# Two decode layers on one core: the MLP in thirds of 1536 columns, with other load orders around it

## The chip, the cores and the metric

The kernel runs on one core of a Trainium2 chip. The metric is the time of one execution on the device in microseconds (us), as the median of several runs. Besides the timed runs there is one profiled execution, from which the trace and the page of the profile come.

## The reference, cut to what matters

All data is float32. A batch of two tokens passes through attention and MLP, twice, with the same weights and the same key and value caches each time.

```python
# x (2, 1, 576); k_cache, v_cache (2, 32, 8192, 128); wq (576, 4096); wo (4096, 576)
# w_gate, w_up (576, 4608); w_down (4608, 576)
def _A_ref(x):
    q = (x @ wq).reshape(2, 1, 32, 128).transpose(0, 2, 1, 3)
    scores = einsum("bhqd,bhkd->bhqk", q, k_cache) * (128 ** -0.5)
    p = softmax(scores, axis=-1)
    o = einsum("bhqk,bhkd->bhqd", p, v_cache)
    return o.transpose(0, 2, 1, 3).reshape(2, 1, 4096) @ wo

def _B_ref(x):
    g = x @ w_gate
    u = x @ w_up
    return (gelu(g, approximate=True) * u) @ w_down

x = x + _A_ref(layernorm(x));  x = x + _B_ref(layernorm(x))
x = x + _A_ref(layernorm(x));  x = x + _B_ref(layernorm(x))
```

The caches hold 537 MB. Both layers together read 1151.6 MB from HBM: the part of the caches that is kept on the chip from layer 0 to layer 1 is read once.

## The kernel before, in words

One large SBUF tile, `space`, takes all that is loaded. The class `Space` manages it while the program is written: every load is a row of `sp.queue` with a key, a place and a length, and `pump` issues the next load on SP's queue as soon as its place holds nothing that is still wanted. `done(key)` marks a load as used and pumps. So the loads come strictly in the order of `sp.queue`, and a load that has to wait for room holds up all that stand behind it. At most eight loads are in flight.

Most of the time is attention over the cache. Layer 0 takes the heads forward, first in pairs, then the last two heads singly; layer 1 takes them backward. For each, DVE multiplies keys by the query (L602), POOL halves the products (L607), DVE reduces them (L621), ACT exponentiates (L674), and PE sums the exponentials (L687) and applies the values (L703).

Two rings in `space` serve the weights. `mid = sp.ring(MID, MIDEND)` has 6912 floats on each partition; through it go, in this order, layer 0's output weights (`out_rows`, 16 loads of 128x1152), its gate and up weights, its down weights, and layer 1's query weights. `big = sp.ring(0, END)` covers the whole tile and serves layer 1's MLP.

The weights that multiply the state (wq, w_gate, w_up) have 576 rows, of which four loads (NW) bring 128 each and a `middle` load brings the 64 that are left. In the MLP the 4608 columns are treated in two halves, and each half in two parts `s`, with 1152 columns to a load (L157, 4608 bytes in a run). `products` (L840) multiplies a block by the state, four matmuls of 288 columns to four 32-row groups of a PSUM bank. `middles` (L189) loads the 64 middle rows of gate and up to alternate partitions of one block, so both are multiplied at once. `hidden` transposes the sums on DVE (L851), applies the norm to them and forms the GELU (L860 to L872). `lower` (L879) multiplies rows of the down weights by it into the PSUM tile `xps`. The down weights come in pieces of some rows each: two rows a load in layer 0 (`first_down`, L200; every ninth row goes with that of the next quarter, L203), and 9, 9, 5, 4, 4, 2, 1, 1, 1 rows in layer 1 (`last_down`). Between the last of these pieces PE does a few products that no result needs (`idle`, L923).

At the end of layer 0's attention `project` (L747) multiplies the output weights, in pieces of two rows. One piece, `early`, stands on PE ahead of the last item's softmax:

```python
early = pieces[:1] if n == last and layer == 0 else []
for piece in early:
    project(*piece)
softmax(n)
total(n)
values(n, pieces[1:9] if n == last and layer == 0 else ())
```

At the start of layer 1 `turn` (L402) transposes the new state, and the query matmuls (L459, L475) run as the query weights land: first those of the last heads, 256 columns (`last_heads`, L169), then two halves in turn. At the end of the program the state is added (L929) and stored (L931).

Of the kernel before, what the change touches and what calls it, by code (L numbers as in the profile page):

```python
# [15 lines left out]
P = 128  # L16
B = 2
# [16 lines left out]
CF = HF // 4  # L34
BF = CF // 2
NI = 9
NT = 4
# [70 lines left out]
def decode_layers(ctx, tc, x_in, kc, vc, wq, wo, wg, wu, wd, out):  # L108
# [74 lines left out]
    def middles(key, where, half, lo=0, hi=HF):  # L183

        def load(a):
            at_of[key] = a
            for r, w in enumerate((wg, wu)):
                src = bass.AP(w.tensor, w.offset + (8 + half) * HF + lo, [[18 * HF, HALF], [1, hi - lo]])
# [49 lines left out]
    idle = {(1, NT - 2, 0): (256, 256), (1, NT - 2, 5): (256, 256, 256), (1, NT - 1, 0): (160,)}  # L238
# [52 lines left out]
    for k in range(1, 4):  # L291
# [3 lines left out]
    cache("k", 1, s0, LATE, 0, 1)  # L295
# [19 lines left out]
    for half in range(2):  # L315
        middles(("m", 1, half), big, half)
# [129 lines left out]
    def attention(layer, items, apart):  # L446
# [25 lines left out]
        else:  # L472
# [7 lines left out]
            nc.vector.memset(qsb[96:P, TAIL:], 0.0)  # L480
            at = at_of["wq", 1, "t"]
# [3 lines left out]
            norm(apart)  # L485
# [3 lines left out]
            qlast = once.tile([P, CT], F32, name="qlast")  # L489
            nc.scalar.activation(qlast, qp[1][:, 0:CT], AF.Copy)  # L490
            apart4 = once.tile([P, 4, B], F32, name="apart4")
            nc.vector.tensor_mul(
                apart4, chosen[:, 1:2, :].to_broadcast([P, 4, B]), quarter.unsqueeze(2).to_broadcast([P, 4, B])
            )
# [23 lines left out]
        def rest_of_queries():  # L518
            for i in range(NW):
# [236 lines left out]
        if layer == 1:  # L756
            body(0)
            body(1)
# [8 lines left out]
        for n in range(last + 1):  # L767
# [4 lines left out]
            for k, unit in enumerate(units):  # L772
# [8 lines left out]
                if k == 0:  # L781
# [6 lines left out]
                    if first:  # L788
                        query(1)
                        first_of_queries()  # L790
                        rest_of_queries()
                    elif n < last:
                        query(n + 1)
                else:
                    add_up(*pending)
                    if k == 1 and layer == 1 and n == 1:
# [10 lines left out]
            if eager(n):  # L807
# [18 lines left out]
        for piece in pieces[9:] if layer == 0 else [(g,) for g in order[3:-1]]:  # L826
# [5 lines left out]
    def mlp(layer, apart):  # L832
        banks = (acc, qp) if layer else ((acc[1], qp[1]), (sm[1], acc[1]))
        done_first = set()

        def products(half, s, lhs, at, stop):
            for c in range(4):
                key = half, s, c
                lo = at + c * BF
                nc.tensor.matmul(  # L840
                    banks[half][s][32 * c:32 * c + WIN, 0:BF], lhs, space[:, lo:lo + BF],
                    start=key not in done_first, stop=stop,
                )
                done_first.add(key)
# [3 lines left out]
        def hidden(half):  # L848
            t = once.tile([P, 2, NI, 32], F32, name="turned", tag="row")
            for s in range(2):  # L850
                nc.vector.transpose(t[:, s, :, :], banks[half][s][:, 0:BF].rearrange("p (j k) -> p k j", k=NI))  # L851
            rows_ = t.rearrange("p s k w -> p (s k) w")[:, :, 0:WIN].rearrange("p t (g r) -> p t g r", g=2)
            shape = [P, 2 * NI, 2, B]
            n = 2 * NI * B
# [11 lines left out]
            h = hT[half] = work.tile([P, 2 * NI, B], F32, name="hT")  # L866
# [7 lines left out]
        def lower(piece):  # L874
            key = ("d", layer) + piece[0]
            for k, (t, i) in enumerate(piece):
                for c in range(4):
                    a = at_of[key] + k * D + c * CW
                    nc.tensor.matmul(  # L879
                        xps[32 * c:32 * c + B, 0:CW], hT[t // 2][:, t % 2 * NI + i, :], space[:, a:a + CW],  # L880
# [5 lines left out]
        if layer == 0:  # L886
            for half in range(2):
                for g, name in enumerate("gu"):
                    for i in range(NW):
                        for s in range(2):  # L890
                            key = name, 0, half, i, s
                            products(half, s, window(g, i), at_of[key], False)
                            done(key)
                        if half == g == i == 0:
# [64 lines left out]
```

## Time and profile before

| what | value |
|---|---|
| median of 3 runs | 2686.24 us (2685.68 to 2686.43) |
| profiled execution, its own time | 2687.66 us |
| its span | 2685.9 us |
| busy share of PE, DVE, ACT, POOL | 35%, 69%, 7%, 43% |
| bytes read from HBM | 1151.60 MB, 429 GB/s over the span |
| share of SP's queue in 16 DMA engines | 99.7% |
| granted TensorE clock, mean | 0.627 |

The span runs from the first to the last recorded instruction; 1.8 us of the execution's time lie outside it. In a row of the page or of the tables, "x8" is a count of instructions, "DMA share" is the mean busy share of the core's 16 DMA engines, and the bracket at the end of a row of the timeline gives how long the engine had been idle and what released it. Layer 0's MLP lies between 1293 and 1370 us of the span, layer 1's from about 2600 us to the end.

### The profile page before, as it was taken

To read this page: it belongs to the slowest core of one execution; us is meant where nothing else is said; L and a number is where in the kernel's file an instruction comes from. 1 tells how busy PE (TensorE), PEld (TensorE's weight loads), DVE (VectorE), ACT (ScalarE), POOL (GpSimd) and SP (SyncE) were. 2 spreads that over 40 slices of the span, in tenths; PEclk is the share of its full clock that TensorE was granted. 3 is DMA by queue.
4 is the path that set the end of the run, shared out by engine and by line. 5 is a ranking of instruction groups with operands and counts; after the bars stand their busy time and mean duration, and the time that the engine had idled before them with its cause. 6 is when DMAs were issued, how large, how long until landed. Compare 5 with 4: busy or idle time off the path is not lost.

```text
span 2685.9 us, 18299 instructions
## 1 busy us (share of the span) xinstructions
PE 940.4 (35%) x7230; PEld 321.6 (12%) x7230; DVE 1863.2 (69%) x1349; ACT 180.5 (7%) x918; POOL 1144.0 (43%) x342
## 2 busy tenths in 40 slices
PE   2332332333233323325764233233323332332346
PEld 0110111011001101102121011001100110111022
DVE  5578777867777687787158777776787778777750
ACT  0000000000000000003013100000000000000000
POOL 2345444544554454453024444554454445445530
PEclk7656665666566566656676566566566656665677
DMA  9999999999999999999999999999999999999998
GB/s 422 435 437 428 434 433 435 434 434 431 432 433 435 434 433 433 431 431 419 407 399 436 433 434 435 433 435 427 436 433 435 432 436 429 434 434 438 426 428 373
DMA packets 38598, 1152.80 MB, mean 429 GB/s; under 512 B 4320, under 2 KB 4976, under 8 KB 17136
## 3 DMA queue, kind: packets, MB, share of 16 engines
q1 hardware_dynamic: 38488, 1151.62, 99.7%
q8 instruction: 57, 0.93, 0.1%
q14 instruction: 29, 0.24, 0.0%
q10 hardware_dynamic: 24, 0.01, 0.0%
HBM read 1151.60 MB, written 0.00 MB: 429 GB/s over the span
## 4 chain that ended last, share of the span: by engine, by line
DMA 26%; DVE 12%; PE 8%; POOL 7%; ACT 1%; issue 1%; POOLq 0%; SPq 0%; ACTq 0%; DVEq 0%
DMA space<-in_A_k_cache_dram 18%; DVE space L602 7%; POOL space L607 7%; PE acc L703 6%; DVE S L621 4%; DMA space<-in_B_w_down_dram 3%; DMA space<-in_A_v_cache_dram 2%; DMA space<-in_B_w_gate_dram 1%; DMA space<-in_B_w_up_dram 1%; DMA space<-in_A_wo_dram 1%; DVE osb L720 1%; ACT prz L674 1%; DMA space<-in_A_wq_dram 1%; PE sm L665 0%; PE sm L684 0%
## 5 line engine op out<-in xcount | busy, mean ns | idle before, releaser
L607 POOL TENSOR_TENSOR space<-space 128x2048 f32<-128x2048 f32 (+3 forms) x332 | 1140.5, 3443 | 1313.9 <-DVE space L602 1180.7
L602 DVE TENSOR_TENSOR space<-space,qp 128x4096 f32<-128x4096 f32 (+2 forms) x329 | 1127.0, 3441 | 462.0 <-DMA space<-in_A_k_cache_dram 451.9
L621 DVE TENSOR_REDUCE S<-space 128x32 f32<-128x2048 f32 (+3 forms) x332 | 582.0, 1753 | 114.9 <-POOL space L607 111.9
L703 PE MATMUL acc<-space,prz 128*8 128x512 f32 x4096 | 593.5, 742 | 7.8 <-issue 6.5
L731 PE MATMUL spare<-weights,osb 128*64 128x2 f32 (+1 forms) x528 | 70.8, 256 | 1198.8 <-ACT osb L722 1181.2
L731 PEld LDWEIGHTS spare<-weights,osb 128*64 128x64 f32 (+1 forms) x528 | 65.2, 208 | 1215.2 <-ACT osb L722 1196.2
L703 PEld LDWEIGHTS acc<-space,prz 128*8 128x8 f32 x4096 | 115.3, 103 | 420.6 <-issue 416.0
L658 PE MATMUL sm<-ident,m 128*1 128x128 f32 x68 | 24.7, 363 | 331.7 <-DVE m L656 331.7
L722 ACT COPY osb<-osb 128x128 f32<-128x128 f32 x60 | 17.9, 298 | 1728.9 <-DVE osb L720 1728.9
L720 DVE SCALAR_TENSOR_TENSOR osb<-acc,diag,osb 128x128 f32<-128x128 f32 x204 | 71.6, 351 | 7.2
L429 POOL TENSOR_TENSOR rstd<-ve,mhalf 128x2 f32<-128x2 f32 x4 | 2.8, 699 | 166.1 <-DVE ve L428 166.1
L684 PE MATMUL sm<-rs,one 128*128 128x2 f32 x120 | 34.8, 360 | 81.1 <-ACT prz L674 81.1
L611 ACT ACTIVATE space<-space 128x128 f32<-128x128 f32 x188 | 55.6, 297 | 69.7 <-DVE space L602 54.8
L674 ACT ACTIVATE prz<-S,nbs 64x128 f32<-64x128 f32 (+1 forms) x136 | 53.3, 392 | 3.1
L665 PE MATMUL sm<-m,one 1*128 1x2 f32 (+1 forms) x136 | 39.0, 354 | 23.0 <-DVE m L663 23.0
L658 PEld LDWEIGHTS sm<-ident,m 128*1 128x1 f32 x68 | 5.4, 79 | 342.4 <-DVE m L656 311.4
L840 PE MATMUL acc<-space,xt 128*6 128x288 f32 x256 | 30.1, 584 | 30.3 <-DMA space<-in_B_w_gate_dram 15.0
L684 PEld LDWEIGHTS sm<-rs,one 128*128 128x128 f32 x120 | 29.7, 307 | 86.3 <-ACT prz L674 86.3
L663 DVE TENSOR_REDUCE m<-sm 1x2 f32<-1x128 f32 (+1 forms) x68 | 18.9, 278 | 30.1 <-PE sm L658 30.1
L851 DVE STREAM_TRANSPOSE turned<-acc 128x288 f32<-128x288 f32 x4 | 1.9, 483 | 52.9 <-PE acc L840 52.9
L665 PEld LDWEIGHTS sm<-m,one 1*128 1x128 f32 x136 | 33.1, 301 | 41.5 <-DVE m L663 41.3
L670 ACT ACTIVATE nbs<-sm 128x2 f32<-128x2 f32 (+1 forms) x68 | 11.7, 172 | 388.5 <-PE sm L665 388.5
(126 smaller groups left out, 432.1 us busy)
## 6 DMA issues: line engine op xcount, KB each, us to landing
space<-in_A_k_cache_dram SPq DMA_DIRECT2D x8, 4096.0 KB, 19.5
space<-in_A_v_cache_dram SPq DMA_DIRECT2D x3, 4096.0 KB, 30.0
space<-in_A_v_cache_dram SPq DMA_DIRECT2D x6, 2048.0 KB, 32.2
space<-in_B_w_down_dram SPq DMA_DIRECT2D x19, 576.0 KB, 7.4
space<-in_B_w_gate_dram SPq DMA_DIRECT2D x18, 576.0 KB, 7.4
space<-in_B_w_up_dram SPq DMA_DIRECT2D x18, 576.0 KB, 7.8
space<-in_A_wo_dram SPq DMA_DIRECT2D x16, 576.0 KB, 8.1
space<-in_A_wo_dram SPq DMA_DIRECT2D x8, 1152.0 KB, 24.0
```

Of the source, the lines that this page charges most:

```text
L602: nc.vector.tensor_tensor(out=u, in0=t, in1=qp_of(n)[:, 0:DH].unsqueeze(1).to_broadcast([P, r1 - r0, DH]), op=ALU.mult)
L607: nc.gpsimd.tensor_tensor(out=half, in0=half, in1=u[:, :r2 - r0, DH // 2:], op=ALU.add)
L611: nc.scalar.activation(row, row, AF.Copy, accum_out=S[n][:, 16 * lo + r:16 * lo + r + 1])
L621: nc.vector.tensor_reduce(out=S[n][:, r0:r1], in_=half, axis=AX.X, op=ALU.add)
L658: nc.tensor.transpose(peaks[n], m, ident)
L665: nc.tensor.matmul(low[n], one[0:1, :].to_broadcast([1, P]), m1, start=True, stop=True)
L674: nc.scalar.activation(prz[rows_, 0:item.rows // 4, e, :], s[rows_, 0:item.rows].rearrange("p (g r) -> p g r", r=4), AF.Exp, bias=nbs[rows ...
L684: nc.tensor.matmul(tot, ones, rs[:, n % 2, :], start=True, stop=True)
L703: nc.tensor.matmul(acc_of(n)[32 * c:32 * c + 8, :], prz[:, g, :, :].rearrange("p e r -> p (e r)"), space[:, at:at + 4 * DH], start=(g < 4) ...
L720: nc.vector.scalar_tensor_tensor(t, q[:, r, :], diag[:, r:r + 1], t, op0=ALU.mult, op1=ALU.add)
L731: nc.tensor.matmul(to[:, i, 0:item.heads], t[:, i:item.heads * DH:GH], w, start=True, stop=True,)
L840: nc.tensor.matmul(banks[half][s][32 * c:32 * c + WIN, 0:BF], lhs, space[:, lo:lo + BF], start=key not in done_first, stop=stop,)
```

## The change

The MLP's columns are taken in three thirds of 1536, each with one PSUM bank, instead of two halves with two banks each. `products` makes four matmuls of 384 columns. `hidden` runs three times in a layer, each with one transpose. Layer 0's gate and up loads have 1536 columns (6144 bytes in a run), its down loads three rows (6912 bytes). Layer 1 loads its middle rows in one key of two loads, and its down weights in pieces of 12, 6, 6, 5, 3, 2, 1, 1 rows; the products between them stand behind the third, fourth and fifth piece. The rings keep their sizes.

Around the MLP three orders change. On PE the output weights' early piece is gone, and the pieces go between the groups of values as 3, 2, 2, 1 instead of 2, 2, 2, 2. In layer 1 the last heads' query weights come behind the first two loads of the body instead of ahead of them, and their products likewise (`tail_queries` behind `body(0)`). One part of the first item's keys is loaded ahead of the last two query loads, and the part that lies in the ring goes ahead of two parts of the next item.

```diff
-NI = 9
-NT = 4
+NT = 3
+NI = 12
+TF = DF // NT
+BF = TF // 4
...
-first_down = []
-for t in (0, 2):
-    for k in range(2):
-        first_down += [run(t + k, lo, lo + 2) for lo in range(0, NI - 1, 2)]
-    first_down.append([(t, NI - 1), (t + 1, NI - 1)])
-last_down = [run(t, 0, 9) for t in range(NT - 2)] + [run(NT - 2, *r) for r in ((0, 5), (5, 9))]
-last_down += [run(NT - 1, *r) for r in ((0, 4), (4, 6), (6, 7), (7, 8), (8, 9))]
+first_down = [run(t, lo, lo + 3) for t in range(NT) for lo in range(0, NI, 3)]
+last_down = [run(*r) for r in ((0, 0, 12), (1, 0, 6), (1, 6, 12), (2, 0, 5), (2, 5, 8), (2, 8, 10), (2, 10, 11), (2, 11, 12))]
...
-for half in range(2):
+for t in range(NT):
     for name, w in (("g", wg), ("u", wu)):
         for i in range(NW):
-            for s in range(2):
-                rows((name, 0, half, i, s), w, HF, mid, (2 * i + half) * HF + s * CF * 2, CF * 2)
-    for s in range(2):
-        middles(("m", 0, half, s), mid, half, s * CF * 2, (s + 1) * CF * 2)
+            rows((name, 0, t, i), w, HF, mid, 2 * i * HF + t * TF, TF)
+    middles(("m", 0, t), mid, t * TF, (t + 1) * TF)
...
-last_heads(("wq", 1, "t"), mid)
-middle(("wq", 1, "tm"), wq, HQ, mid, HQ - TAIL, HQ)
 for half in (1, 0):
     for i in range(NW):
...
+        if half and i == 0:
+            last_heads(("wq", 1, "t"), mid)
+            middle(("wq", 1, "tm"), wq, HQ, mid, HQ - TAIL, HQ)
+        if half == 0 and i == NW - 2:
+            cache("k", 1, s0, LATE, 1, 2)
...
-for k in range(1, 4):
+for k in (2, 3, 0):
     cache("k", 1, s0, LATE, k, k + 1)
 for k in range(2, 4):
     cache("k", 1, s1, home[("k",) + s1.name], k, k + 1, MORE if k == 2 else 0)
-cache("k", 1, s0, LATE, 0, 1)
...
+    counts = [3, 2, 2, 1]
...
-            for piece in between[:2]:
+            count = counts.pop(0) if counts else 0
+            for piece in between[:count]:
                 project(*piece)
-            between = between[2:]
+            between = between[count:]
...
 if layer == 1:
     body(0)
+    tail_queries()
     body(1)
...
-        early = pieces[:1] if n == last and layer == 0 else []
-        for piece in early:
-            project(*piece)
         softmax(n)
         total(n)
-        values(n, pieces[1:9] if n == last and layer == 0 else ())
+        values(n, pieces[:8] if n == last and layer == 0 else ())
...
-    banks = (acc, qp) if layer else ((acc[1], qp[1]), (sm[1], acc[1]))
+    banks = (acc[0], acc[1], qp[0]) if layer else (acc[1], qp[1], sm[1])
...
-            nc.tensor.matmul(sm[0][0:B, 0:n], hT[1][:, 0, :], flat[:, 0:n], start=True, stop=True)
+            nc.tensor.matmul(sm[0][0:B, 0:n], hT[0][:, 0, :], flat[:, 0:n], start=True, stop=True)
```

The first place where this moves instructions is SP's list of loads from the end of layer 0's MLP to the first keys of layer 1. Before, it stands as follows (`space` is the large tile, the names behind the arrow are the tensors in HBM, the shapes count partitions and floats).

```order
L200 DMA space<-in_B_w_down_dram 128x1152 x8
L203 DMA space<-in_B_w_down_dram 128x2x576
L200 DMA space<-in_B_w_down_dram 128x1152 x8
L203 DMA space<-in_B_w_down_dram 128x2x576
L169 DMA space<-in_A_wq_dram 64x4x256 x2
L179 DMA space<-in_A_wq_dram 128x1x256
L157 DMA space<-in_A_wq_dram 128x1x1024
L157 DMA space<-in_A_wq_dram 128x1x768
```

Now it stands so, with the end of the query weights behind the mark.

```order
L200 DMA space<-in_B_w_down_dram 128x1728 x12
L157 DMA space<-in_A_wq_dram 128x1x1024
L157 DMA space<-in_A_wq_dram 128x1x768
L169 DMA space<-in_A_wq_dram 64x4x256 x2
L179 DMA space<-in_A_wq_dram 128x1x256
...
L157 DMA space<-in_A_wq_dram 128x1x1024 x6
L147 DMA space<-in_A_k_cache_dram 128x2048
L157 DMA space<-in_A_wq_dram 128x1x1024 x2
L147 DMA space<-in_A_k_cache_dram 128x2048 x3
```

Eighteen down loads have become twelve, the three loads for the last heads have moved behind the first two loads of the body, and one load of keys has moved ahead of the last two of the query weights.

The second place is PE at the last item of layer 0's attention, where `m` holds the maximum, `rs` the sums of the exponentials, `prz` the exponentials and `oT` the outputs of earlier heads. Before:

```order
L665 MATMUL sm_126<-m_2811,one 128x1
L747 MATMUL xps<-space,oT 2x144 x8
L687 MATMUL sm_126<-rs,one 128x1 x2
L703 MATMUL acc_122<-space,prz 8x512 x4
L747 MATMUL xps<-space,oT 2x144 x16
L703 MATMUL acc_122<-space,prz 8x512 x4
L747 MATMUL xps<-space,oT 2x144 x16
```

And now, where the lines of these operations are L661, L745, L683 and L700:

```order
L661 MATMUL sm_126<-m_2811,one 128x1
L683 MATMUL sm_126<-rs,one 128x1 x2
L700 MATMUL acc_122<-space,prz 8x512 x4
L745 MATMUL xps<-space,oT 2x144 x24
L700 MATMUL acc_122<-space,prz 8x512 x4
L745 MATMUL xps<-space,oT 2x144 x16
```

The eight products that stood ahead of the softmax's sums have moved behind the first group of values.

The third place is PE's end, from the last gate and up block on: `hT` is the hidden state, `sm_125` takes the products that no result needs. Before:

```order
L879 MATMUL xps<-space,hT 2x144 x92
L923 MATMUL sm_125<-prz,hT 2x256 x2
L879 MATMUL xps<-space,hT 2x144 x16
L923 MATMUL sm_125<-prz,hT 2x256 x3
L879 MATMUL xps<-space,hT 2x144 x16
L923 MATMUL sm_125<-prz,hT 2x160
L879 MATMUL xps<-space,hT 2x144 x20
```

And now:

```order
L875 MATMUL xps<-space,hT_6499 2x144 x48
L875 MATMUL xps<-space,hT_6512 2x144 x48
L916 MATMUL sm_125<-prz,hT_6499 2x256 x2
L875 MATMUL xps<-space,hT_6525 2x144 x20
L916 MATMUL sm_125<-prz,hT_6499 2x256 x2
L875 MATMUL xps<-space,hT_6525 2x144 x12
L916 MATMUL sm_125<-prz,hT_6499 2x160
L875 MATMUL xps<-space,hT_6525 2x144 x16
```

The 144 products stay; the first 96 stand ahead of the first group of unneeded ones, and that of three is now one of two.

More of the change, by code (lines that the diff above doesn't have):

```diff
@@ L33 @@
 CQ = HQ // 4
-CF = HF // 4
-BF = CF // 2
-NI = 9
-NT = 4
+NT = 3
+NI = 12
+TF = DF // NT
+BF = TF // 4
 CW = D // 4
@@ L181, in middle, with middles @@
         sp.queue.append((key, where, size, load))
-    def middles(key, where, half, lo=0, hi=HF):
+    def middles(key, where, lo=0, hi=DF):
         def load(a):
@@ L795, in attention @@
                     add_up(*pending)
+                    if k == 1 and first:
+                        rest_of_queries(range(1, NW))
                     if k == 1 and layer == 1 and n == 1:
@@ L832, in mlp, with products, hidden @@
     def mlp(layer, apart):
-        banks = (acc, qp) if layer else ((acc[1], qp[1]), (sm[1], acc[1]))
+        banks = (acc[0], acc[1], qp[0]) if layer else (acc[1], qp[1], sm[1])
         done_first = set()
-        def products(half, s, lhs, at, stop):
+        def products(t, lhs, at, stop):
             for c in range(4):
-                key = half, s, c
                 lo = at + c * BF
                 nc.tensor.matmul(
-                    banks[half][s][32 * c:32 * c + WIN, 0:BF], lhs, space[:, lo:lo + BF],
-                    start=key not in done_first, stop=stop,
+                    banks[t][32 * c:32 * c + WIN, 0:BF], lhs, space[:, lo:lo + BF],
+                    start=(t, c) not in done_first, stop=stop,
                 )
-                done_first.add(key)
+                done_first.add((t, c))
         hT = {}
[L848 to L854, printed above, removed]
+        def hidden(t):
+            turned = once.tile([P, NI, 32], F32, name="turned", tag="row")
+            nc.vector.transpose(turned, banks[t][:, 0:BF].rearrange("p (j k) -> p k j", k=NI))
+            rows_ = turned[:, :, 0:WIN].rearrange("p t (g r) -> p t g r", g=2)
+            shape = [P, NI, 2, B]
+            n = NI * B
             mine = once.tile([P, 5 * n], F32, name="mine", tag="osb")
@@ L910, in mlp @@
             several("g", 0, 4, 4)
-            for half in range(2):
-                for s in range(2):
-                    products(half, s, both, at_of["m", 1, half] + s * CF * 2, False)
-                done(("m", 1, half))
+            for t in range(NT):
+                products(t, both, at_of["m", 1] + t * TF, False)
+            done(("m", 1))
             for off, n in ((0, 4), (4, 2), (6, 2)):
                 several("u", 1, off, n)
-            for half in range(2):
-                hidden(half)
+            for t in range(NT):
+                hidden(t)
         flat = prz.rearrange("p g e r -> p (g e r)")
```

58 lines of the change are left out of this document (28 added, 30 removed).

## The prediction

> **What bounds the kernel now.** I read the page's slices and queues first, then a table of windows by stage, then the chain of waits at the two seams between stages, and last the timeline of the end.
>
> ```profile
> span 2685.9 us, 18299 instructions
> ...
> DMA  9999999999999999999999999999999999999998
> GB/s 422 435 437 428 434 433 435 434 434 431 432 433 435 434 433 433 431 431 419 407 399 436 433 434 435 433 435 427 436 433 435 432 436 429 434 434 438 426 428 373
> ...
> q1 hardware_dynamic: 38488, 1151.62, 99.7%
> q8 instruction: 57, 0.93, 0.1%
> ```
>
> One queue, q1, fills 99.7% of the time of 16 DMA engines over the span, and no slice but the last falls below nine tenths. No compute engine is near that. So the time is the time in which the bytes come in, and the bytes do not change. Only three things can move it: how fast a load runs, when the queue has nothing to carry, and what follows the last byte. The rate dips in slices 19 to 21, where layer 0 ends, so the windows go there (busy time of PE, PEld, DVE, ACT and POOL, then granted clock, DMA share, GB/s).
>
> ```profile
> 400.00:1000.00 600.00, 183.17 (x1215) 61.69 (x1215) 447.60 (x279) 26.38 (x120) 288.12 (x79) 0.61 1.00 433
> 1272.00:1276.00 4.00, 4.00 (x47) 1.79 (x50) 0.33 (x2) 0.00 (x0) 0.00 (x0) 0.59 0.85 328
> 1290.00:1345.00 55.00, 39.66 (x335) 6.43 (x330) 6.03 (x27) 0.39 (x2) 0.70 (x1) 0.62 1.02 411
> 1345.00:1370.00 25.00, 18.01 (x280) 6.55 (x272) 2.06 (x9) 0.23 (x1) 0.00 (x0) 0.64 1.03 405
> 1370.00:1380.00 10.00, 8.20 (x119) 3.55 (x118) 4.89 (x19) 0.50 (x2) 0.69 (x1) 0.62 0.99 372
> 2657.00:2675.00 18.00, 12.60 (x200) 6.81 (x204) 4.88 (x20) 0.47 (x2) 0.00 (x0) 0.62 1.00 420
> 2675.00:2680.00 5.00, 5.00 (x104) 3.05 (x96) 0.00 (x0) 0.00 (x0) 0.00 (x0) 1.00 0.61 239
> 2680.00:2685.90 5.90, 1.88 (x41) 0.56 (x40) 0.31 (x1) 0.00 (x0) 0.00 (x0) 0.92 0.06 20
> ```
>
> Attention loads, in long runs, come at 433 GB/s. Layer 0's gate and up weights (1290 to 1345) come at 411 and its down weights at 405, with the DMA share still at 1.02 and 1.03: the engines are occupied and slower, not waiting. Only one window shows the queue short of work, 1272 to 1276 at 0.85, which is 0.6 us. In the last windows the share is 0.61 and 0.06: the 16 engines run out of work several microseconds apart.
>
> **The change part by part.** *Longer runs.* In 1293 to 1338 the queue carries almost nothing but 4608-byte runs:
>
> ```profile
> DMA packets 4543, 18.51 MB, mean 411 GB/s; under 512 B 533, under 2 KB 533, under 8 KB 4539
> ```
>
> At 411 GB/s over 16 engines such a run takes one engine 4608·16/411000 = 0.1794 us; at 433 it would take 0.1703. The difference, 9.1 ns, I charge to each run as a fixed part. Runs removed: gate and up of layer 0, 32·128 + 8·64 = 4608 become 24·128 + 6·64 = 3456, so 1152; its down weights, 16·128 + 2·256 = 2560 become 12·128 = 1536, so 1024; layer 1's middle rows 4·64 become 2·64, so 128; its down pieces 9·128 become 8·128, so 128. Together 2432 runs, times 9.1 ns, over 16 engines: **1.4 us less**. The bounds: nothing, if the low rate comes from something other than runs; and 3.9 us, if all 31.9 MB of layer 0's MLP (3·4608·576·4 bytes) went at 433 instead of 411 (77.5 less 73.6 us). I take 1.4, since runs only grow by a third and a half.
>
> The Trainium skill, "DMA: Bandwidth & Descriptors", section "Why small descriptors are slow", puts about three bus cycles on each packet beside one for every 32 bytes, which is 3 in 147 for 4608 bytes, 2.0%. The rows above show 5%; by the page the term would be an estimated 0.55 us instead of 1.4.
>
> *Fewer instructions.* Products keep their columns (four of 288 become three of 384), so PE's time on them stays, in a quarter fewer instructions: eight a block for 72 blocks become eight for 54, 144 fewer, and as many weight loads. The page's 18299 instructions against 57 fetch packets are about 320 for one, so about one fetch goes. A packet costs one engine of sixteen 0.1%·16·2686/57 = 0.75 us, and matters only on the engine that ends last. I take **0.2 us less**, between 0 and 0.75. The third `hidden` adds some ten short operations to each MLP; in layer 0 they run beside loads, and the first third's are done long before a down weight lands.
>
> *The four-block ring.* Layer 0's loads wait until the oldest block in the ring is used. Six blocks of 1152 floats fitted; now four of 1536 do (768 floats stay empty), and four of 1728. The next rows are the landing time of the gate and up loads, their issue on SP, and PE's work, a row for each block.
>
> ```profile
> DMA to landing us min/median/max: 7.1/7.5/7.9
> ...
> L157 SPq DMA_DIRECT2D space<-in_B_w_gate_dram x16: 534/535/552, 1285.7 to 1322.4; - x16
> ...
> 1302.50 1.12 PE L840 MATMUL acc<-space,xt 128*6 128x288 f32 x8 [1.08 <-DMA space<-in_B_w_gate_dram]
> 1303.93 1.15 PE L840 MATMUL qp<-space,xt 128*6 128x288 f32 x8 [0.31 <-DMA space<-in_B_w_gate_dram]
> ...
> 1308.22 0.67 PE L840 MATMUL acc<-space,xt 128*6 128x288 f32 x8 [0.76 <-DMA space<-in_B_w_up_dram]
> ```
>
> A block lands every 1.43 us (1302.50 to 1303.93) and takes PE 0.67 to 1.15 us, so 0.9 to 1.53 for 1536 columns. A round of four new blocks lasts 4·0.786 MB at 411 GB/s = 7.65 us; the queue runs dry if one block's turn needs more: PE's 1.53, the issue's 0.53, and the landing of a load with little ahead of it. Of the six blocks five were in flight when the median load took 7.5 us, four of them ahead: 7.5 − 4·1.43 = 1.8 us, and 0.5 more for the larger block, so a need of 4.4 us. A lone load is not in the trace. The shortest landing among the output weights, where the queue ran low, bounds it from above:
>
> ```profile
> DMA to landing us min/median/max: 4.9/8.1/14.1
> ```
>
> With 4.9 + 0.5 the need is 7.5, still just within 7.65. I am nearer to the 4.4, because it comes from the same loads, and take 0 (the slow side is the first rival). One place is tighter: the first down block covers the room of two gate or up blocks, so both must be used, and the budget there is two blocks and its own 2.1 us, 5.9 us. Against 4.4 to 7.5 that loses 0 to 1.6; I take **0.3 us more**.
>
> *Output weights before the softmax.* Before, PE took one piece of the output weights ahead of the last softmax and sat waiting for its load:
>
> ```profile
> 1267.77 0.18 ACT L674 ACTIVATION_READ_ACCUMULATOR prz<-S,nbs 64x1 f32 x1
> 1270.37 1.14 PE L747 MATMUL xps<-space,oT 128*2 128x144 f32 x16 [3.56 <-DMA space<-in_A_wo_dram]
> 1271.44 1.01 PE L687 MATMUL sm<-rs,one 128*128 128x1 f32 x4
> 1272.38 1.89 PE L703 MATMUL acc<-space,prz 128*8 128x512 f32 x8
> ```
>
> The exponentials are there at 1267.95. Now the sums and the first values can start then and end near 1270.9, so three pieces, at 1.14 us, free their room at about 1272.0, 1273.2 and 1274.3; before, the first was free at 1271.5 and the next two only after 1274. That can fill the 0.6 us of the window 1272 to 1276. But a mean share over 16 engines that finish microseconds apart at the end (0.61) need not be time of the last engine: I take **0.2 us less**, between 0 and 0.6.
>
> *Query weights and keys.* The 256-column loads of the last heads now come behind the first two body loads, and one part of the keys goes ahead of the last two query loads. The body loads need `turn` from the finished MLP just as the last heads did:
>
> ```profile
> 1371.96 0.42 DVE xt L402
> 1372.42 1.04 PE qp L475 x32
> ...
> 1379.63 8.17 DMA space<-in_A_wq_dram
> ```
>
> The window 1370 to 1380 has a share of 0.99, 0.1 us to win; its 372 GB/s comes from 1 KB runs, which stay. The keys' new place gives SP something to issue while the last two blocks are used, but the key part that lies in the ring now stands ahead of the others; it may wait for PE's last queries. Cover: two 1 MB parts ahead of it, 4.8 us at 433. I take 0, from −0.2 to +2.4 (one part's time).
>
> *The end.* Three `hidden` instead of two now stand ahead of the last down pieces, and fewer idle products keep PE's clock up.
>
> ```profile
> 2657.93 0.48 DVE L851 STREAM_TRANSPOSE turned<-acc 128x288 f32<-128x288 f32 x1 [32.84 <-PE acc L840]
> 2664.23 0.20 DVE L872 SCALAR_TENSOR_TENSOR hT<-mine 128x36 f32<-128x36 f32 x1
> ...
> 2669.52 6.14 PE L879 MATMUL xps<-space,hT 128*2 128x144 f32 x112 [2.55 <-DMA space<-in_B_w_down_dram]
> ...
> 2682.09 0.43 PE L879 MATMUL xps<-space,hT 128*2 128x144 f32 x8 [0.27 <-DMA space<-in_B_w_down_dram]
> 2682.58 0.31 DVE L929 TENSOR_TENSOR x<-xps,x 128x144 f32<-128x144 f32 x1 [18.16 <-PE xps L879]
> ```
>
> Two `hidden` took 2657.93 to 2664.43, so three end by about 2667.7. PE does 112 products in 6.14 us, 55 ns each, and a row of weights is eight. The down weights, 36 rows of 0.295 MB, land at 420 GB/s in 0.70 us a row, and PE needs 0.44. The first 12 rows, in one load, land some 8.4 us after the last up weights; the other 24 come in over 16.8 us and need 10.6 of PE, so it has caught up before the end. What follows the last landing stays: one row, eight products of 0.43, an add, the store. I take 0; if the clock falls, the last two rows cost up to 0.43 each once more, 0.9 us.
>
> **The sum.** −1.4 − 0.2 + 0.3 − 0.2 = −1.5 us. The profiled execution took 2687.66 us, 1.8 beyond its span; less 1.5 it is 2686.2. The median of the runs, 2686.24, lies 1.42 below that execution, so the forecast for the median is **2684.7**.
>
> **The rivals.** *The ring of four starves (slower).* If the true need is above 7.65 us, every round of four among the 27 gate and up blocks and 12 down blocks, about ten rounds, loses the excess. At 8.0 it is 3.5 us, and with the seam's 1.6 instead of 0.3 the sum is +3.3: 2689.5. At 8.4 it is +7.3: 2693.5. For it: four blocks instead of six, and a need bounded only by 7.5. Against: the estimate of 4.4 from the same loads, and a share of 1.02, in which nothing waits now. It decides from 7.65 us on.
>
> *The bytes run at full pace (faster).* If the low rate of this stage is due wholly to its short loads and the new ones reach 433, the longer runs bring 3.9 instead of 1.4, the window at 1272 its 0.6, the seam costs 0 and the fetch 0.75: −5.2 to −5.5 us, 2680.9. For it: 433 is what long runs get in every attention window. Against: 4608 to 6144 bytes is only a third.
>
> *Each load holds the queue (faster by far).* If a fixed part of each load lay bare, 19 fewer loads (10 of gate and up, 6 and 1 of down, 2 of middle rows) would bring 19 times that part. By the rows the part is at most 1.43 − 0.590 MB/433 = 0.07 us, so 1.3 us in place of the 1.4 above, not beside it: 2684.8. The Trainium skill, "DMA: Bandwidth & Descriptors", section "Anatomy of one DMA", has about 2.0 us fixed for each DMA, which would be an estimated 38 us here if none of it overlapped. The blocks that land 1.43 us apart show that it overlaps.
>
> *It lands on other engines (no change).* The mean rate rises, but the DMA engine that ends last gains nothing, since it carries the fetches; then only the seam's +0.3 or so is left: 2686.5.
>
> **How the numbers follow.** Forecast, from −3.1 to 0: 0.55. No change: 0.12. Starved ring: 0.20, half of it beyond +5.4. Full pace: 0.11. Bare loads: 0.02. The larger part of these two lies near or beyond −5.4 only with gains that no row shows, so I put 0.09 there. About 0.2%, 5.4 us, is what a measurement of this kernel can tell from no change: faster 0.09, same 0.81, slower 0.10. The range leaves out a tenth at either side: from 2680.9, where every gain is full, to 2690.0, a starved ring with a need of 8.05 us.
>
> **What would show it.** Right: in the windows of layer 0's MLP the share stays at 1.00 or more, and the rate rises from 411 and 405 to some 416 to 419; PE's sums at the last softmax start before the output weights land; the chain's last items are one row, the add and the store. Wrong: a share below 0.97 between the first gate block and the last down block (the ring starves; look at the first down load), a rate still at 411 (not the runs), or landing times of the larger loads well above 8 us; and at the end, products of 0.43 us for a row that run on after the last landing in more than one row.

## The result and the profile after

The changed kernel takes 2691.59 us, the median of 19 runs (2689.76 to 2697.04), against 2686.43 us before (19 runs, 2685.68 to 2688.13). That is 5.2 us more, where 1.5 less was forecast, and above the range. The ratio of the mean times is 1.0022, with a 95% interval of 1.0015 to 1.0028. The times also spread three times as far as before.

The profiled execution of the changed kernel took 2689.76 us, the least of its runs. A second profiled execution, of 2692.81 us, is the last experiment below, and both are read here. First the page's rate, in 40 slices of the span of the first one:

```profile
DMA  9999999999999999999999999999999999999998
GB/s 421 436 435 430 432 432 435 434 431 434 431 433 431 435 434 435 430 428 417 391 399 439 429 435 431 434 433 430 435 434 432 429 436 434 431 434 430 433 426 379
```

The largest difference from before is in the slice behind 417, which has 391 instead of 407: the end of layer 0. No other slice differs by more than 8. The DMA line shows nothing there. The windows of that place in the first profiled execution are the gate and up stage, the down stage, and the seam between them:

```profile
1290.00:1345.00 55.00, 37.60 (x250) 5.05 (x242) 7.06 (x34) 0.60 (x3) 0.71 (x1) 0.59 1.00 386
1345.00:1370.00 25.00, 15.13 (x244) 6.32 (x248) 2.03 (x9) 0.22 (x1) 0.00 (x0) 0.71 1.00 397
1344.00:1349.00 5.00, 3.23 (x20) 0.26 (x16) 0.16 (x1) 0.00 (x0) 0.00 (x0) 0.66 0.89 303
```

Before, the seam had no gap:

```profile
1344.00:1349.00 5.00, 3.45 (x52) 1.11 (x52) 2.54 (x10) 0.23 (x1) 0.00 (x0) 0.70 1.02 413
```

Gate and up fell from 411 to 386 GB/s while the share stayed at 1.00, and at the seam the share fell to 0.89. The chain of waits inside the gate and up stage shows what a block waits for:

```profile
1298.65 7.33 DMA space<-in_B_w_up_dram
1305.97 0.04 issue
1306.02 1.51 PE acc L837 x8
1307.53 0.02 issue
1307.55 6.50 DMA space<-in_B_w_gate_dram
1314.05 0.04 issue
1314.09 1.51 PE qp L837 x8
```

A load lands, PE uses the block, at that moment a new load is issued into its room, and so on: a closed loop of 6.50 + 0.04 + 1.51 + 0.02 = 8.07 us a round. Four blocks of 0.786 MB at the 411 GB/s of before would take 7.65. Read so, the loads come as fast as the loop allows, not as fast as the engines could; the experiments test this reading.

To see where the time goes over the whole run, I added up the bytes of the transfer records in both traces and compared the moments at which the same amount had landed (columns four to six are experiments below: "thirds only" is the MLP's part of the change alone, "five blocks" and "best" are the experiments with five blocks of 1536, with three-row and with two-row down loads).

```
MB landed, about what          before, us   later than before, us:
                                            changed  again  thirds only  five blocks  best
548  layer 0's output weights  1270.2       +0.1     +0.2   +0.2         +0.0         +0.0
556  first gate loads          1291.2       -0.3     -0.4   +0.4         -0.6         -0.5
576  last up loads             1340.0       +2.9     +4.0   +5.2         -0.5         -0.6
580  first down loads          1349.7       +4.3     +6.9   +7.7         +0.6         -0.6
588  last down loads           1369.4       +4.0     +6.3   +7.4         +0.7         -0.8
600  first keys of layer 1     1400.9       +2.7     +5.9   +5.6         -0.0         -2.5
1150 last but one MB           2674.5       +2.7     +5.8   +5.6         -0.0         -2.6
```

The first profiled execution loses 3.2 us in gate and up and 1.4 at the seam and wins 0.4 at the output weights and 1.3 at the query weights. The second loses 4.4 and 2.9 and wins 0.6 and 0.4. Outside these places no row moves against the one above by more than 0.6 us. The column of before is one execution, of 2687.66 us, 1.2 above its median, so what all columns win against it at one place may be its own loss.

### The profile page after: what moved, and what is told of

Same layout as the page of the kernel before. It is cut to its first block, busy times and chain, and to the rows that moved or that the text cites. A ratio compares the mean times of both kernels' runs of the same rounds, so it can differ in the third digit from the quotient of the medians.

```text
span 2687.9 us, 17986 instructions
## 1 busy us (share of the span) xinstructions
PE 942.7 (35%) x7084; PEld 318.8 (12%) x7084; DVE 1865.1 (69%) x1363; ACT 181.0 (7%) x920; POOL 1143.8 (43%) x342
## 4 chain that ended last, share of the span: by engine, by line
DMA 25%; DVE 14%; PE 8%; POOL 6%; issue 1%; ACT 1%; POOLq 0%; SPq 0%; DVEq 0%; ACTq 0%
DMA space<-in_A_k_cache_dram 18%; DVE space L598 8%; POOL space L603 6%; PE acc L700 6%; DVE S L617 4%; DMA space<-in_B_w_up_dram 3%; DMA space<-in_B_w_down_dram 2%; DMA space<-in_A_v_cache_dram 1%; DVE osb L718 1%; DMA space<-in_B_w_gate_dram 1%; ACT prz L670 1%; DMA space<-in_A_wq_dram 1%; DMA space<-in_A_wo_dram 1%; PE xps L745 0%; PE sm L661 0%
## 5 line engine op out<-in xcount | busy, mean ns | idle before, releaser
L700 PE MATMUL acc<-space,prz 128*8 128x512 f32 x4096 | 596.3, 745 | 8.1 <-issue 6.7
L700 PEld LDWEIGHTS acc<-space,prz 128*8 128x8 f32 x4096 | 113.6, 103 | 424.3 <-issue 419.7
L661 PE MATMUL sm<-m,one 1*128 1x2 f32 (+1 forms) x136 | 39.1, 355 | 23.0 <-DVE m L659 23.0
L716 DVE TENSOR_SCALAR osb<-acc,diag 128x128 f32<-128x128 f32 x68 | 23.2, 342 | 23.2 <-PE acc L700 23.2
L661 PEld LDWEIGHTS sm<-m,one 1*128 1x128 f32 x136 | 33.3, 302 | 41.6 <-DVE m L659 41.4
L837 PE MATMUL acc<-space,xt 128*6 128x384 f32 x192 | 27.2, 684 | 25.6 <-DMA space<-in_B_w_up_dram 15.6
```

Of the source, the lines that this page charges most:

```text
L661: nc.tensor.matmul(low[n], one[0:1, :].to_broadcast([1, P]), m1, start=True, stop=True)
L700: nc.tensor.matmul(acc_of(n)[32 * c:32 * c + 8, :], prz[:, g, :, :].rearrange("p e r -> p (e r)"), space[:, at:at + 4 * DH], start=(g < 4) ...
L837: nc.tensor.matmul(banks[t][32 * c:32 * c + WIN, 0:BF], lhs, space[:, lo:lo + BF], start=(t, c) not in done_first, stop=stop,)
```

## The experiments

Theory A: four blocks are too few, and the loads wait for room. Theory B: the longer runs are slower in themselves. Theory C: the changed orders cost the time. Times are medians, and ratios are of mean times, to runs of the kernel before on the same chip, with 95% intervals. The runs of the changed kernel spread over 7 us, so medians that differ from its own by 0.5 us or less do not tell a kernel from it.

**The orders alone.** Before's MLP with the three changed orders, beside the other lines of the change that belong to them:

```diff
-                early = pieces[:1] if n == last and layer == 0 else []
...
+            tail_queries()
             body(1)
...
+            if half == 0 and i == NW - 2:
+                cache("k", 1, s0, LATE, 1, 2)
```

> Before's MLP (six blocks of 1152 columns in the ring, two-row down loads) with the three changed orders alone: output weights behind the softmax, last heads' query weights behind two body loads, one key part ahead of the last two query loads. Theory A (the ring of four blocks is too short for a block's turn) and theory B (6144-byte runs are slower in themselves) both expect what the bytes over time show for the orders in the changed kernel: about 0.4 us gained at the output weights and 0.5 to 1.3 at the query weights, so 1 to 2 us below before, and gate and up at 411 GB/s as before. Theory C (the orders cost the time) expects 3 to 5 us above before.

Measured: 2686.86 us against 2686.45, ratio 1.0001 (0.9992 to 1.0010). C falls. The expected gain of 1 to 2 us did not come either. In the profile this kernel is 1.0 us early at the first gate loads, gives 0.7 of it back over the next 20 us of gate loads, and wins 0.9 at the query weights. The profiled execution of before was itself 1.2 us above its median, so such a gain on paper is no gain in the time. At the query weights this is plain: the kernels with the orders of before win there too, 1.8 us with the thirds alone and 1.2 and 1.0 with before's ring of four and of five blocks.

**The thirds alone.** The changed MLP with the orders of before.

```diff
-NI = 9
-NT = 4
+NT = 3
+NI = 12
...
+                rows((name, 0, t, i), w, HF, mid, 2 * i * HF + t * TF, TF)
+        middles(("m", 0, t), mid, t * TF, (t + 1) * TF)
```

> The changed kernel's MLP with the orders of before. A and B expect the loss without the orders' gain: 5 to 7 us above before, gate and up at about 386 GB/s, and a gap at the first down load. C expects the time of before within 1 us.

Measured: 2692.91 us against 2686.45, ratio 1.0023 (1.0013 to 1.0032). The loss is the MLP's, 5.2 us of it by the last up loads and 2.5 at the seam.

**Before with four blocks.** The sizes of before, but the ring of gate and up cut.

```diff
+    four = sp.ring(MID, MID + 8 * D)
...
-                    rows((name, 0, half, i, s), w, HF, mid, ...)
+                    rows((name, 0, half, i, s), w, HF, four, ...)
```

> The kernel before, all loads of the same size, but the gate and up loads of layer 0 go round four blocks of 1152 columns instead of six. A: a round lasts 4 x 1.43 = 5.7 us, and a block's turn needs PE's 0.7 to 1.15, the issue's 0.54 and a lone load's landing, 4.1 to 4.9 us (the first down load of the changed kernel took about that), so 5.4 to 6.6 us: each of nine rounds loses 0 to 0.9 us, 2 to 8 us above before, gate and up at 380 to 400 GB/s. B: the runs are the same, so the time of before and 411 GB/s.

Measured: 2700.94 us, 14.5 us above before, ratio 1.0052 (1.0040 to 1.0065). Its chain and its transfers between 1296 and 1340 us:

```profile
1306.41 1.19 PE qp L841 x8
1307.60 0.02 issue
1307.62 6.33 DMA space<-in_B_w_up_dram
1313.95 0.04 issue
1314.00 1.19 PE qp L841 x8
```

```profile
DMA packets 3468, 14.13 MB, mean 321 GB/s; under 512 B 409, under 2 KB 409, under 8 KB 3464
```

With 4608-byte runs and PE's work as before, the stage falls from 411 to 321 GB/s. This chain's round is 7.58 us; by the rate, 4·0.590 MB at 321 GB/s, it is 7.35 on average. The direction is A's, and B expected nothing; the loss is nearly twice A's upper figure, because the landing in the chain takes 6.33 us and not 4.1 to 4.9. Four such blocks at 411 GB/s would take 5.74 us, and nine rounds that each lose 7.35 − 5.74 come to 14.5.

**A quarter of the products.**

```diff
             for c in range(4):
+                if layer == 0 and c and not stop and (t, c) in done_first:
+                    continue
```

> The changed kernel with only one of the four column groups of each gate and up block of layer 0 multiplied, but for the first and the last block of each third; the loads are the same. A: PE's part of a block's turn falls from 0.9 to 1.5 us to 0.2 to 0.4, the turn fits into the round of 7.5 us, gate and up go at 415 to 420 GB/s, and the time falls 2 to 4 us below the changed kernel. B: the rate stays at 386 and the time is that of the changed kernel.

This kernel leaves out three of the four products of most blocks. Measured: 2691.31 us, the time of the changed kernel, with 379 GB/s between 1296 and 1340 us. This looks like B, but PE's row of one block shows that the run did not test what it should:

```profile
1315.82 1.45 PE L839 MATMUL qp<-space,xt 128*6 128x384 f32 x2 [0.41 <-DMA space<-in_B_w_gate_dram]
```

The one product left, two instructions, takes 1.45 us; the four products of a block, eight instructions, take 1.47 in the changed kernel. The four column groups run side by side, and leaving out three saves nothing.

**A quarter of the columns.**

```diff
+                few = BF // 4 if layer == 0 and not stop and (t, c) in done_first else BF
...
-                    banks[t][32 * c:32 * c + WIN, 0:BF], lhs, space[:, lo:lo + BF],
+                    banks[t][32 * c:32 * c + WIN, 0:few], lhs, space[:, lo:lo + few],
```

> The changed kernel, but each product of a gate and up block of layer 0 takes 96 of its 384 columns, except for the first and the last block of each third. In the run with a quarter of the products a block still took PE 1.45 us, the four column groups having run side by side, so that run had not shortened PE's turn; this one does, to some 0.25 to 0.4 us. Theory A (the ring): a round of four needs 8.15 us in the changed kernel (4 blocks of 0.786 MB at 386 GB/s), of which about 1.1 us goes; 7.05 us is under the 7.26 of 433 GB/s, so gate and up go at 411 to 425 GB/s and the time falls 2.5 to 4 us below the changed kernel. Theory B (long runs are slow in themselves): 386 GB/s and the time of the changed kernel.

This kernel leaves out three quarters of the columns of most blocks. Measured: 2691.05 us, 0.5 below the changed kernel where A expected 2.5 to 4; the time does not tell it from the changed kernel.

```profile
1316.31 0.51 PE L838 MATMUL qp<-space,xt 128*6 128x96 f32 x8 [1.35 <-DMA space<-in_B_w_gate_dram]
```

```profile
1290.00:1345.00 55.00, 21.07 (x251) 4.77 (x253) 7.06 (x34) 0.60 (x3) 0.71 (x1) 0.50 1.00 398
```

PE's part fell by 0.96 us and the rate rose, but only to 398; over gate and up the trace loses 1.5 us, where the first profile of the changed kernel lost 3.2. The seam, whose blocks keep their full work, loses 2.0. So a shorter turn of PE's did not bring the full rate. Had the landing stayed at 6.50 us, the round would have been 7.1 us and the ring long enough. The landings in its chain took 6.1 to 7.9 us instead, and what sets them no run shows.

**Half blocks.** Gate and up in loads of 768 columns, nine to the ring.

```diff
-                rows((name, 0, t, i), w, HF, mid, 2 * i * HF + t * TF, TF)
+                for s in range(2):
+                    rows((name, 0, t, i, s), w, HF, mid, 2 * i * HF + t * TF + s * TF // 2, TF // 2)
```

> The changed kernel with each gate and up load of layer 0 cut into two of 768 columns (3072 bytes in a run); nine of them fit into the ring. A: a round of nine lasts 9 x 0.95 = 8.6 us against a need below the 7.35 us that four blocks of 1152 showed, so nothing starves; what is left is the price of short runs, 395 to 408 GB/s, and the gap at the first down load shrinks; 1 to 3 us below the changed kernel, though the runs are half as long. B (a size of its own at fault) has no forecast; if short loads were the cost, this would be 2 us or more above the changed kernel.

Measured: 2690.16 us, 1.4 below the changed kernel, ratio to before 1.0014 (1.0005 to 1.0022); with 393 GB/s between 1296 and 1340 us. Loads with runs half as long are faster here than the longer ones, which speaks against B. How much of what is missing to 411 is the price of the short runs was not separated. A new loss of 2.4 us came at the query weights; its cause was not followed up.

**Two-row down loads.**

```diff
-    first_down = [run(t, lo, lo + 3) for t in range(NT) for lo in range(0, NI, 3)]
+    first_down = [run(t, lo, lo + 2) for t in range(NT) for lo in range(0, NI, 2)]
```

> The changed kernel with layer 0's down weights in two-row loads of 1152 floats, six to the ring. A: the first down load needs only one block's room, so the gap of 1.4 us at the seam goes; the down stage keeps 405 GB/s or more; 1 to 2 us below the changed kernel. If the seam is only a shift of the same wait, the time stays.

Measured: 2691.18 us, 0.4 below the changed kernel, ratio 1.0018 (1.0009 to 1.0027), and the seam still loses 2.5 us. With four blocks ahead of it the seam is short of loads with either size of the first down load.

**Fillers for PE's clock.**

```diff
                         done(key)
+                        for n in (160, 160):
+                            nc.tensor.matmul(sm[0][0:B, 0:n], flat[:, 0:B], flat[:, 0:n], start=True, stop=True)
```

> The changed kernel with two unneeded products of 160 columns behind each gate and up block of layer 0, so that PE waits less and its clock rises from 0.59. A: PE's turn of a block falls from 1.45 towards 0.9 us, the need from 8.15 to about 7.6 us, gate and up go at 400 to 411 GB/s, 1 to 3 us below the changed kernel, and the times spread less. If the clock stays low, the unneeded products stand in the way of the next block and the time rises by 1 to 5 us. B: no change.

Measured: 2689.83 us, 1.8 below the changed kernel, ratio 1.0012 (1.0003 to 1.0021). The clock rose to 0.89 in the stage:

```profile
1290.00:1345.00 55.00, 39.83 (x343) 13.66 (x341) 7.06 (x34) 0.60 (x3) 0.71 (x1) 0.89 1.00 387
```

The time came as expected, the rate did not: 387 GB/s. As with the quarter of the columns, PE's turn got shorter (0.87 us in the chain) and the rate hardly moved. Inconclusive as to where the 1.8 us came from.

**Five blocks of 1536.** The room is taken from keys kept between the layers.

```diff
-MORE = 8 * DH
-END = 24 * PART + 768 + MORE
+MORE = 2 * DH
+END = 24 * PART + 768 + 8 * DH
```

> The changed kernel with a ring of 7680 floats instead of 6912, so that five blocks of 1536 columns fit. The room comes from keys of one head that were kept from layer 0 to layer 1: 768 floats a partition more are read in layer 1, 0.39 MB, 0.9 us. Loads, runs and PE's work of the MLP are the same. A (the ring): a round of five lasts 9.1 to 9.4 us against the 8.15 us that four took, so nothing starves, gate and up go at 411 to 421 GB/s, and the time falls 3 to 6 us below the changed kernel, to 2686 to 2688. B (6144-byte runs are slow in themselves): 386 GB/s and 0 to 2 us above the changed kernel.

Measured: 2688.35 us (2687.68 to 2689.43), 3.2 below the changed kernel, though it reads 0.39 MB more; ratio to before 1.0007 (0.9999 to 1.0016). Its transfers between 1296 and 1340 us, and its chain:

```profile
DMA packets 3361, 18.18 MB, mean 413 GB/s; under 512 B 406, under 2 KB 406, under 8 KB 3357
```

```profile
1307.20 8.04 DMA space<-in_B_w_gate_dram
1315.24 0.04 issue
1315.28 0.88 PE qp L837 x8
1316.16 0.02 issue
1316.17 8.47 DMA space<-in_B_w_up_dram
```

The same loads with the same runs go at 413 GB/s as soon as there is room for a fifth. B falls. Five blocks last 9.5 us at this rate, more than the loop of about 8 needed in the ring of four, so a block's room is free in time. Against the profile of before, what is left of the loss is 1.1 us at the seam.

**Before with five blocks.** The third experiment with `MID + 10 * D`.

> The kernel before with the gate and up loads of layer 0 in a ring of five blocks of 1152 columns. A: with four blocks the stage ran at 321 GB/s, a block in 1.84 us, so the turn of a block takes 7.35 us; five blocks at full pace last 7.15 us, just less: 1 to 4 us above before, gate and up at 395 to 405 GB/s. B: the time of before.

Measured: 2689.47 us, 2.9 above before, ratio 1.0010 (1.0002 to 1.0019). Its transfers between 1296 and 1340 us:

```profile
DMA packets 4187, 17.05 MB, mean 388 GB/s; under 512 B 493, under 2 KB 493, under 8 KB 4183
```

The price falls with the blocks as A says: 14.5 us at four, 2.9 at five, none at six. In bytes of room, the rings of both block sizes fall into one order: 321 GB/s at 2.36 MB (four small blocks), 388 at 2.95 (five small), 386 and 374 at 3.15 (four large, the two profiles), 411 at 3.54 (six small), 413 at 3.93 (five large).

**Five blocks and two-row down loads.**

> The kernel with five blocks of 1536, and layer 0's down weights in two-row loads, of which six fit. A: beside the gain of the five blocks the seam between up and down weights has one more load in flight, so its gap of 1.4 us goes; 0 to 1.5 us below the kernel with five blocks and three-row loads, 2685 to 2687. If the seam's gap comes from the spread of the 16 engines, which both kernels have, no difference.

Measured: 2685.72 us (2685.22 to 2686.74) against 2686.56 for before; ratio 0.9997 (0.9988 to 1.0006). It is 2.6 below the kernel with three-row loads, more than expected, and the lowest median of all, but the interval does not tell it from before. Its windows of gate and up, down, and the seam show no gap:

```profile
1290.00:1345.00 55.00, 34.02 (x256) 4.58 (x254) 7.06 (x34) 0.60 (x3) 0.70 (x1) 0.72 1.01 412
1345.00:1370.00 25.00, 17.43 (x292) 6.83 (x288) 2.03 (x9) 0.22 (x1) 0.00 (x0) 0.68 1.02 408
1344.00:1349.00 5.00, 4.02 (x56) 1.15 (x48) 2.03 (x9) 0.22 (x1) 0.00 (x0) 0.68 1.02 405
```

**The changed kernel once more.** No edit.

> The changed kernel once more, for a second profiled execution: the first one took 2689.76 us, the least of its 19 runs, 1.8 below their median. A: a longer execution loses its further time where the first lost its own, between the first gate block and the second down load, at a rate of 386 GB/s or less in the gate and up stage, and nowhere else by more than 0.5 us. If the further time is lost in the attention stages or at the end, the ring explains only part.

Measured: one execution of 2692.81 us. The same three windows:

```profile
1290.00:1345.00 55.00, 35.76 (x234) 4.49 (x237) 7.06 (x34) 0.60 (x3) 0.70 (x1) 0.59 0.99 379
1345.00:1370.00 25.00, 15.99 (x216) 5.77 (x208) 2.03 (x9) 0.22 (x1) 0.00 (x0) 0.57 0.96 368
1344.00:1349.00 5.00, 3.56 (x24) 0.39 (x24) 0.00 (x0) 0.00 (x0) 0.00 (x0) 0.50 0.82 288
```

Of its 3.1 us beyond the first profiled execution, 1.2 are lost in gate and up and 1.5 at the seam; the query weights win 0.9 less, which does not fit the expectation's 0.5, and the down weights 0.3 more. One difference at the seam can be seen. Of the two blocks that the first down load waits for, the second took PE 0.83 us in the first execution and 1.47 in this one, at the lower clock. Rows of the first, then of the second:

```profile
1343.47 0.83 PE L837 MATMUL sm<-space,xt 128*6 128x384 f32 x8 [1.50 <-DMA space<-in_B_w_up_dram]
```

```profile
1344.57 1.47 PE L837 MATMUL sm<-space,xt 128*6 128x384 f32 x8 [1.64 <-DMA space<-in_B_w_up_dram]
```

At this place the later end of PE's turn delays the first down load. It does not explain gate and up: between 1296 and 1340 us four blocks took 0.83 in the second execution and two in the first, and the second was the slower. What makes the wide spread of the changed kernel stays open.

## Why the prediction was wrong

**The four-block ring is the step that failed.** The prediction took 0 for the stage, from a need of 4.4 us, bounded by 7.5, against a budget of 7.65. The need measured 8.07 in the chain, 8.15 by the rate. The subtraction 7.5 − 4·1.43 took the landing time for the loads ahead and a small rest of 1.8 us. With two loads ahead it gives 4.7 us for the old block size and 6.1 for the new. The landing times between 1296 and 1340 us, first in the changed kernel, then in before with four blocks:

```profile
DMA to landing us min/median/max: 6.1/6.4/6.7
DMA to landing us min/median/max: 5.1/6.4/6.6
```

In the rings of four the landing did not shrink to this; in before with five blocks it did, 5.9 us where the subtraction gives 6.1. In the changed kernel 0.3 us too much is enough, since at the full rate a landing of 6.1 us and PE's 1.5 already fill the 7.65. Taking the need from a load with nothing ahead hid how close this was. What keeps a landing at 6.4 us in a ring of four is open. The bound failed too. The shortest landing, 4.9 us, was of a smaller load in another stage, and gate and up loads in the short ring took 6.4. The first rival had this mechanism and its price: at 8.0 us it gave 2689.5, at 8.4 2693.5. By the same working the measured 8.07 to 8.15 give 2690.2 to 2691.0, and the measured time is 2691.59. The rival was given 0.20.

**The seam**, 0.3 us with a bound of 1.6, measured 1.4 and 2.9 in the two profiles. Its reason was half right. Two blocks must be used first, but a first down load that needs only one did not close the gap in the ring of four (2.5 us), and a fifth block did not with three-row loads (1.1); both together did.

**The sign for a starved ring was half right.** It wanted a share below 0.97, and at the first down load, where it said to look, the share was 0.89 and 0.82. But in gate and up, where the larger part was lost, it was 1.00 and 0.99, and the landings, 6.1 to 7.6 us in the two profiles, stayed below the 8 of the other sign. In the transfer records the median 6144-byte packet takes 234 ns in the changed kernel and 236 in the best one. But of the 2752 packets between 1296 and 1340 us, 127 are stretched by over 30%, up to 2.1 us, and their excess comes to 3.4 us for each of 16 engines; in the best kernel it is 0.4. In before with four, five and six blocks it is 6.0, 2.4 and 0.1 us. So the share most likely counts an engine's wait for the next load as a long packet; the records do not show it directly.

**Longer runs**, −1.4 us, are not shown clear of the scatter of profiles. Where the ring does not starve, 6144-byte runs reach 413 and 415 GB/s between 1296 and 1340 (the two kernels with five blocks), 4608-byte ones 411 (before) and 405 (the orders alone). For the down weights between 1350 and 1366, 6912-byte runs reach 418 in the changed kernel and 405 in the one with five blocks, against 409. At the best of these, 415 and 418, the 21.2 and 10.6 MB would gain 0.5 and 0.6 us, 1.1 together with nothing for layer 1's pieces, so 1.4 was somewhat large; the Trainium skill's three cycles a packet ("DMA: Bandwidth & Descriptors", "Why small descriptors are slow"), an estimated 0.55 us, are about half of this 1.1.

**Fewer instructions**, −0.2 us: the page has 17986 instructions and 55 fetch packets after 18299 and 57, so two fetches went and not one. What they brought was not measured by itself.

**Fewer loads.** The gain of 1.3 us in the rival in which each load holds the queue was not tested apart from that of the longer runs. The 2.0 us that it quotes from the Trainium skill ("DMA: Bandwidth & Descriptors", "Anatomy of one DMA") stand there for transfers issued by GpSimd; these loads are issued by SP, and no run here measures a fixed time for one.

**Output weights.** The sums start at 1269.17 instead of 1271.44, ahead of the landing:

```profile
1269.17 1.04 PE L683 MATMUL sm<-rs,one 128*128 128x1 f32 x4 [0.73 <-ACT prz L670]
1270.15 1.89 PE L700 MATMUL acc<-space,prz 128*8 128x512 f32 x8
1271.81 2.52 PE L745 MATMUL xps<-space,oT 128*2 128x144 f32 x48
```

The gain was 0.4 and 0.6 us in the two profiles, inside 0 to 0.6, and the three kernels with the old order have none. But the window that it was to fill, 1272 to 1276, still has a share of 0.87 (0.85 before). At the **query weights** 1.3 and 0.4 us were won, where 0 was taken and 0.2 was the bound; since kernels with the old orders win 1.0 to 1.8 at the same place, this is not shown to be the orders' doing. Alone, the orders gave nothing that the times show. **The end** came as said, one row, an add and the store behind the last landing:

```profile
2684.27 0.47 PE xps L875 x8
2684.74 0.02 issue
2684.76 0.31 DVE x L922
```

## What to carry to other kernels

Before making loads larger in a ring of fixed size, count the blocks and the bytes of room that stay in use (here 3.15 of 3.54 MB), and compare what they last at the full rate with the loop's time (landing, use, issue of the next) from the chain of waits. A landing time measured in a full queue, less the loads ahead, was no measure of what the shorter queue needed; cutting the ring of the old kernel by one or two blocks measures the margin directly (2.9 and 14.5 us here), and adding a block tests the cause.

## What the runs showed of the hardware

Two things were unexpected. A DMA share of 1.00 can hide a starved queue: 386 and 412 GB/s stood beside shares of 1.00 and 1.01, and of these two the rate alone told them apart; the stretched packets say where the difference lies. And four products to four 32-row groups of a PSUM bank took the time of one: 1.45 us for two instructions of one group, 1.47 for eight instructions of all four, both at a granted clock of 0.50, while cutting the columns from 384 to 96 brought 0.51.
